# Linear attention and two MLPs: weights split once, their parts kept in DRAM, and the leaky ReLU taken by ScalarE out of PSUM

## The chip, the core and the metric

The kernel runs on one core of a Trainium2 chip. The metric is the device time of one execution in microseconds (us); lower is better. The engines have short names in all rows: PE is TensorE (matmuls), PEld its weight loads, DVE is VectorE, ACT is ScalarE, POOL is GpSimd, and SPq is the queue of SyncE, which issues all of this kernel's DMAs in a fixed order.

## The reference

For 4 batches of 576 tokens the reference does an attention without softmax over 8 heads and then two MLPs, all in float32:

```python
def phi(x):                                   # x: batch, head, 576, 64;  w_phi: 64 x 128
    proj = einsum('bhsd,df->bhsf', x, w_phi)
    proj = proj - max(abs(proj), axis=-1, keepdims=True)
    return concatenate([exp(proj), exp(-proj)], axis=-1)
q_p, k_p = phi(q), phi(k)
kv  = einsum('bhsf,bhsd->bhfd', k_p, v);  z = sum(k_p, axis=2)
x   = einsum('bhsf,bhfd->bhsd', q_p, kv) / (einsum('bhsf,bhf->bhs', q_p, z) + 1e-6)

h   = x @ w_in                                # 512 x 2048
x   = maximum(0.01 * h, h) @ w_out            # 2048 x 512
g   = x @ w_gate                              # 512 x 1536
out = (g / (1 + exp(-g)) * (x @ w_val)) @ w_out2
```

The weights reach the chip as float64.

## The kernel before

**Products in parts.** A float32 product is made of three fast ones: each operand is split into a high part (a rounding to the fast format `F32R`) and a low part (what is left), and high by high, high by low and low by high are added up in PSUM. A split is one ACT copy (the high part) and one DVE subtraction (the low part, `sub`, line 57).

**The two layers as units.** `products` (line 530 is its matmul) makes one unit: 24 matmuls of 128 x 128 by 288 columns, 12 for each half of the tokens of one batch. A batch has 16 units `u_l1` (first layer, one weight of 128 x 512 each), 12 pairs of `u_gate` and `u_val`, and after every four of `u_l1` or four such pairs a group of four units `u_out`, which read the four weights of that group (the sum, into `acc`). That makes 68 units per batch, 68 weights, and 6528 matmuls at line 530 in all. `u_l1` copies its product out of PSUM on ACT (`cp`, line 60), applies the leaky ReLU on DVE (line 554), and splits the result (`to_parts`, tile `gp`).

**A weight's way.** In batch 0 each of the 68 weights is loaded as float64 (`w_load`, line 477, into a buffer of the ring `wi`, which has 5), turned into float32 (`w_to_f32`: two ACT passes at lines 491 and 492, three DVE passes at 493, 494 and 499, into a buffer `wr`), and written to DRAM as float32 (line 504, `kept`). Then `w_split` (line 510 on ACT, line 57 on DVE) makes the two parts, for weights of the first kind again in a buffer of the ring `wi`, for the weights of `u_out` in a ring `wo`. In batches 1 to 3 the float32 copy is read back (line 480) and split again, once in each batch. Eight gate weights are turned into float32 ahead of time (`early`).

**The order.** Attention steps of the next batch are laid between the units of the present one; the first attention runs alone ahead of the first unit. `splits` calls loads, conversions and splits a fixed number of weights ahead. A scheduler then lays every engine's instructions into one fixed list; each engine and the DMA queue work their list strictly in order.

Of the kernel before, what the change touches and what calls it, by code (L numbers as in the profile page):

```python
# [7 lines left out]
F32 = mybir.dt.float32  # L8
# [9 lines left out]
P = 128  # L18
# [8 lines left out]
# blocks of 32 tokens in a half  # L27
NB = HT // 32
# columns of the constants before the signs
NC = P + 18 + NB  # L30
# token tiles of 128 rows; of tile i the first VAL[i] rows are its own, the rest belong to the next
# [3 lines left out]
# on the high word of a float64 read as float32, this takes 896 off the exponent  # L35
# [4 lines left out]
def linear_attention_two_mlps(ctx: ExitStack, tc, qT, kT, vt, w_phi, w1, w2, wg, wv, w3, cst, out):  # L40
# [21 lines left out]
    # ---------------------------------------------------------------- constants  # L62
# [30 lines left out]
    def bk(b=1):  # L93
        """A bank; those of the two layers still lie idle in the first attention's projections."""
        if b == 0:
            return T([P, 512], F32, "pm", 4, psm)
        return T([P, 512], F32, "pa", 4, psa)

    # ---------------------------------------------------------------- attention, keys
# [3 lines left out]
    def whole(b):  # L103
        """While the vector engine is short: whole float32 products in place of split ones."""
        return b < 2

    def lean(b):
        """Past the start, where the vector engine has time: the maxima from turned projections."""
        return b >= 1
# [139 lines left out]
    def k_steps(b):  # L249
        """Steps of the key side; each follows the one before by two on its data."""  # L250
# [32 lines left out]
    # ---------------------------------------------------------------- attention, queries  # L283
# [42 lines left out]
    def q_p(b, j, t):  # L326
        """Projections with features on the partitions, and their largest size by 32 features."""
# [12 lines left out]
    def q_m_t(b, j, t):  # L340
        """The largest over all features, as rows that one product takes off the projections."""
# [97 lines left out]
    def q_steps_t(b):  # L439
        """Steps of the query side: half the tokens of two heads take two for the projections,  # L440
        two for the exponentials and two for the products, one group behind the other."""
# [26 lines left out]
    # ---------------------------------------------------------------- weights  # L468
    wtile, w64, wf = {}, {}, {}
    src = {"1": w1, "2": w2, "g": wg, "v": wv, "3": w3}  # L470
    kept = {}

    def w_load(key, tag="wi", n=5):
        kind, b, f = key
        if b == 0 and (kind, f) not in kept:
            w64[key] = t = T([P, 512, 2], I32, tag, n)
            nc.sync.dma_start(out=t.rearrange("p n t -> p (n t)"), in_=src[kind][f].bitcast(I32))
        else:
            wf[key] = t = T([P, 512], F32, "wr", 4)
            nc.sync.dma_start(out=t, in_=kept[kind, f])  # L480

    def w_to_f32(key):
        """float64 bits to float32: sign, 31 bits, and the rounding, which goes onto the lower 16 bits
        (as they saturate, the step up is left out where all of them are set already)."""
# [4 lines left out]
        t = T([P, 512], F32, "wr", 4)  # L489
# [11 lines left out]
        kind, _, f = key  # L501
        uid[0] += 1
        kept[kind, f] = d = dram.tile([P, 512], F32, name=f"kept_{uid[0]}")
        nc.sync.dma_start(out=d, in_=t)

    def w_split(key):
        kind, b, f = key
        r = wf.pop(key)
        wtile[key] = t = T([P, 2, 512], F32R, *(("wo", 4) if kind in "23" else ("wi", 5)))
        i = act.activation(t[:, 0], r, AF.Copy)  # L510
        tc.stamp_issue_order_token(i.ins, "weights")
        sub(t[:, 1], r, t[:, 0].bitcast(F32))

    def early(key):
        """Weights that are made ready while the first attention runs."""
        w_load(key, "gp", 5)
        w_to_f32(key)
        del wf[key]

    # ---------------------------------------------------------------- the two layers  # L520
    gp, acc, x2h, x2l, sg = ({} for _ in range(5))

    def products(ops):
        """The two halves of the tokens, each in a bank of its own."""
# [25 lines left out]
    def u_l1(b, f):  # L550
        g = T([P, S], F32, "es", 5)
        for c, ps in products(in_ops(("1", b, f), xh, xl, b)):
            cp(g[:, c], ps)
        dve.scalar_tensor_tensor(out=g, in0=g, scalar=0.01, in1=g, op0=ALU.mult, op1=ALU.max)  # L554
# [219 lines left out]
```

## Time and profile before

| | |
|---|---|
| median of 3 runs | 1103.33 us (1102.61 to 1103.87) |
| span of the profiled execution, first to last instruction | 1099.4 us |
| PE busy | 1078.7 us, 98% of the span |
| DVE busy | 854.7 us, 78% |
| ACT busy | 659.9 us, 60% |
| moved by DMA | 130.25 MB, mean 118 GB/s |

The profiled execution has a span alone and no time of its own beside it; the median of the runs is 3.9 us above that span. A busy share is over the whole span. Since PE's matmuls are pipelined and their ends are modelled, PE counts as idle only where no matmul at all is under way.

### The profile page before, as it was taken

The numbers are of one execution on the slowest core, as the hardware profiler recorded it, in microseconds if no ns is written. First come the engines' busy times: TensorE is split into PE (matmuls) and PEld (weight loads), VectorE is DVE, ScalarE is ACT, GpSimd is POOL, SyncE is SP. The second block draws the span as 40 slices with busy tenths as digits, with TensorE's granted clock in tenths as the row PEclk, the third lists the DMA queues.
The fourth block names the chain that finished last, engine by engine and source line by source line (L and its number), as shares of the span: only waits on it lengthen the run. The fifth ranks groups of instructions, "written<-read, shape, count | busy, mean of one in ns | idle before, by whom it ended". The sixth has DMA issues, their size and how long they took to land.

```text
span 1099.4 us, 20402 instructions
## 1 busy us (share of the span) xinstructions
PE 1078.7 (98%) x7728; PEld 1041.9 (95%) x7728; DVE 854.7 (78%) x1765; ACT 659.9 (60%) x1457; POOL 6.8 (1%) x28
## 2 busy tenths in 40 slices
PE   7899999999999999999999999999999999999998
PEld 6668999999998999999999999999999999999998
DVE  6998889898999888779778888878787645565553
ACT  7768877667766787556646576655563444344421
POOL 1000000000000000000000000000000000000000
PEclk9999999999999999999999999999999999999999
DMA  9735766454654532223223322232131232323211
GB/s 332 237 93 174 213 209 194 154 155 155 211 185 125 172 100 91 80 57 110 62 76 108 103 73 89 77 98 97 36 97 51 80 99 77 92 82 106 97 48 44
DMA packets 69329, 130.25 MB, mean 118 GB/s; under 512 B 17136, under 2 KB 17392, under 8 KB 69232
## 3 DMA queue, kind: packets, MB, share of 16 engines
q1 hardware_dynamic: 69232, 128.95, 37.8%
q8 instruction: 61, 1.00, 0.4%
q14 instruction: 36, 0.29, 0.1%
HBM read 106.38 MB, written 22.54 MB: 117 GB/s over the span
## 4 chain that ended last, share of the span: by engine, by line
PE 82%; DVE 5%; DMA 5%; ACT 5%; issue 1%; SPq 0%; ACTq 0%; DVEq 0%
PE pm L530 70%; PE pa L391 4%; DMA wi<-in_w_dram 3%; PE pa L200 3%; PE pa L159 2%; DVE wr L499 1%; DMA wi<-in_wv_dram 1%; DVE wr L494 1%; ACT wr L491 1%; PE pm L299 1%; PE pa L344 1%; ACT wi L492 1%; PE pa L365 1%; PE pa L334 0%; PE pa L335 0%
## 5 line engine op out<-in xcount | busy, mean ns | idle before, releaser
L530 PE MATMUL pm<-xh,wi 128*128 128x288 f32 x2560 | 534.0, 297 | 2.2 <-ACT wi L510 1.6
L530 PEld LDWEIGHTS pm<-xh,wi 128*128 128x128 f32 x2560 | 416.5, 188 | 6.1 <-ACT wi L510 1.8
L530 PE MATMUL pm<-gp,wo 128*128 128x288 f32 x2688 | 385.3, 296 | 2.6 <-ACT acc L60 1.5
L530 PE MATMUL pm<-xl,wi 128*128 128x288 f32 x1280 | 378.9, 297 | 0.0
L530 PEld LDWEIGHTS pm<-gp,wo 128*128 128x128 f32 x2688 | 365.3, 188 | 6.6 <-ACT acc L60 1.8
L530 PEld LDWEIGHTS pm<-xl,wi 128*128 128x128 f32 x1280 | 240.4, 188 | 2.5 <-issue 1.7
L510 ACT ACTIVATE wi<-wr 128x512 fp32r<-128x512 f32 x160 | 101.0, 635 | 59.9 <-PE pm L530 34.6
L57 DVE TENSOR_TENSOR wi<-wr,wi 128x512 fp32r<-128x512 f32 x160 | 108.9, 682 | 14.2 <-ACT wi L510 13.0
L588 DVE TENSOR_TENSOR acc<-pm,acc 128x288 f32<-128x288 f32 x160 | 70.8, 453 | 57.1 <-PE pm L530 56.2
L510 ACT ACTIVATE wo<-wr 128x512 fp32r<-128x512 f32 x112 | 67.2, 630 | 65.5 <-PE pm L530 59.5
L57 DVE TENSOR_TENSOR wo<-wr,wo 128x512 fp32r<-128x512 f32 x112 | 74.3, 682 | 31.0 <-ACT wo L510 30.8
L57 DVE TENSOR_TENSOR gp<-es,gp 128x576 fp32r<-128x576 f32 x112 | 83.8, 749 | 13.5 <-ACT gp L60 12.6
L60 ACT ACTIVATE gp<-es 128x576 fp32r<-128x576 f32 x112 | 76.7, 687 | 25.0 <-DVE es L554 15.6
L561 ACT ACTIVATE es<-pm 128x288 f32<-128x288 f32 x96 | 39.4, 413 | 45.1 <-PE pm L530 44.5
L60 ACT ACTIVATE es<-pm 128x288 f32<-128x288 f32 x128 | 52.5, 417 | 16.5 <-PE pm L530 16.0
L57 DVE TENSOR_TENSOR fl<-ff,fh 128x512 fp32r<-128x512 f32 (+1 forms) x72 | 51.0, 714 | 13.0 <-ACT fh L60 12.7
L569 DVE SCALAR_TENSOR_TENSOR es<-pm,es 128x288 f32<-128x288 f32 x96 | 43.0, 450 | 23.0 <-PE pm L530 22.7
L492 ACT ACTIVATE wi<-wi 128x512 int32<-128x512 uint32 x60 | 41.2, 687 | 32.7 <-DMA wi<-in_w_dram 20.2
L562 DVE SCALAR_TENSOR_TENSOR es<-es,pm 128x288 f32<-128x288 f32 x96 | 42.1, 444 | 20.5 <-ACT es L561 19.9
L554 DVE SCALAR_TENSOR_TENSOR es<-es 128x576 f32<-128x576 f32 x64 | 48.0, 751 | 8.7 <-ACT es L60 8.7
L491 ACT ACTIVATE wr<-wi 128x512 f32<-128x512 f32 x60 | 40.7, 684 | 15.8 <-DMA wi<-in_w_dram 4.7
L394 ACT ACTIVATE dn<-pa 64x288 f32<-64x288 f32 x64 | 26.1, 408 | 37.8 <-PE pa L391 36.8
(108 smaller groups left out, 1282.1 us busy)
## 6 DMA issues: line engine op xcount, KB each, us to landing
wr<-kept SPq DMA_DIRECT2D x212, 256.0 KB, 2.8
wi<-in_w_dram SPq DMA_DIRECT2D x44, 512.0 KB, 4.3
kept<-wr SPq DMA_DIRECT2D x68, 256.0 KB, 4.1
wi<-in_wv_dram SPq DMA_DIRECT2D x12, 512.0 KB, 4.1
raw<-in_kT_dram SPq DMA_DIRECT2D x16, 288.0 KB, 3.1
raw<-in_qT_dram SPq DMA_DIRECT2D x16, 288.0 KB, 3.1
out_dram<-acc SPq DMA_DIRECT2D x16, 288.0 KB, 2.4
gp<-in_wg_dram SPq DMA_DIRECT2D x8, 512.0 KB, 7.8
```

The lines of the kernel that those rows point to most:

```text
L57: dve.tensor_tensor(out=o, in0=a, in1=b, op=ALU.subtract)
L60: act.activation(o, a, AF.Copy)
L391: pe.matmul(ps, w, x, start=(i == 0), stop=(i == len(ops) - 1))
L491: act.activation(t, high.bitcast(F32), AF.Abs, scale=REBIAS)
L492: act.activation(low, low.bitcast(U32), AF.Copy, scale=2.0**-29)
L510: i = act.activation(t[:, 0], r, AF.Copy)
L530: m = pe.matmul(ps, w, x[:, c], start=(i == 0), stop=(i == n - 1))
L554: dve.scalar_tensor_tensor(out=g, in0=g, scalar=0.01, in1=g, op0=ALU.mult, op1=ALU.max)
L561: act.activation(t[:, c], ps, AF.Tanh, scale=0.5)
L562: dve.scalar_tensor_tensor(out=t[:, c], in0=t[:, c], scalar=1.0, in1=ps, op0=ALU.add, op1=ALU.mult)
L569: dve.scalar_tensor_tensor(out=g[:, c], in0=ps, scalar=0.5, in1=g[:, c], op0=ALU.mult, op1=ALU.mult)
L588: dve.tensor_tensor(out=acc[o][:, t], in0=ps, in1=acc[o][:, t], op=ALU.add)
```

## The change

The weights are split only once, in batch 0, and what is written to DRAM is both parts (512 KB) in place of the float32 copy (256 KB). `keep_all_but(2)` writes them with a delay: the parts of a weight are written when two newer ones have been split. Batches 1 to 3 load the parts straight into a buffer of `wi` or `wo`, without a split. (The last two weights of batch 0 are still unwritten when batch 1 asks for them; these two are loaded as float64, converted and split a second time in batch 1.) The ring `wo` grows from 4 to 5 buffers, `wr` shrinks from 4 to 3. The leaky ReLU of `u_l1` becomes the function of the ACT pass that takes the product out of PSUM; the DVE pass is gone.

```diff
@@ weights
+    def parts_tile(key):
+        wtile[key] = t = T([P, 2, 512], F32R, *(("wo", 5) if key[0] in "23" else ("wi", 5)))
+        return t
+    def keep(cols, src_ap):
+        uid[0] += 1
+        d = dram.tile([P, cols], F32, name=f"kept_{uid[0]}")
+        nc.sync.dma_start(out=d, in_=src_ap)
+        return d
+    def keep_all_but(n):
+        while len(unkept) > n:
+            key, t = unkept.pop(0)
+            kept[key[0], key[2]] = keep(1024, flat(t))
     def w_load(key, tag="wi", n=5):
-        kind, b, f = key
-        if b == 0 and (kind, f) not in kept:
+        kind, _, f = key
+        if (kind, f) in kept:
+            nc.sync.dma_start(out=flat(parts_tile(key)), in_=kept[kind, f])
+        elif (kind, f) in ready:
+            wf[key] = t = T([P, 512], F32, "wr", 3)
+            nc.sync.dma_start(out=t, in_=ready[kind, f])
+        else:
             w64[key] = t = T([P, 512, 2], I32, tag, n)
             nc.sync.dma_start(out=t.rearrange("p n t -> p (n t)"), in_=src[kind][f].bitcast(I32))
-        else:
-            wf[key] = t = T([P, 512], F32, "wr", 4)
-            nc.sync.dma_start(out=t, in_=kept[kind, f])
...
     def w_split(key):
-        kind, b, f = key
+        if key not in wf:
+            return
         r = wf.pop(key)
-        wtile[key] = t = T([P, 2, 512], F32R, *(("wo", 4) if kind in "23" else ("wi", 5)))
+        t = parts_tile(key)
         i = act.activation(t[:, 0], r, AF.Copy)
         tc.stamp_issue_order_token(i.ins, "weights")
         sub(t[:, 1], r, t[:, 0].bitcast(F32))
+        unkept.append((key, t))
...
     def u_l1(b, f):
         g = T([P, S], F32, "es", 5)
         for c, ps in products(in_ops(("1", b, f), xh, xl, b)):
-            cp(g[:, c], ps)
-        dve.scalar_tensor_tensor(out=g, in0=g, scalar=0.01, in1=g, op0=ALU.mult, op1=ALU.max)
+            act.activation(g[:, c], ps, AF.Prelu, alpha=0.01)
         to_parts(g, ("1", b, f))
...
             ahead(loaded, w_load, done[0] + 5)
+            keep_all_but(2)
```

The scheduler makes other lists of it. Over the whole program ACT loses 202 splits and gains 2 conversions, DVE loses 202 splits and the 64 leaky passes; ACT has one table load in either list. Up to the last, eighth, low part of the first attention's result (`xl<-xf`) DVE's list held 17 conversions and 5 splits of weights and now holds 14 and 3.

The first place is ACT's list at the end of the first attention. `xh<-xf` takes a piece of its result, `dn` and `ff` are attention, `es<-pm` is the first unit's product; `wr<-wi` and `wi<-wi` convert a weight, `wr<-gp` one of the eight early ones, `wi<-wr` and `wo<-wr` split one. Before:

```order
L60 ACTIVATE xh_635<-xf_660 128x288
L394 ACTIVATE dn_724<-pa_732 64x288
L373 ACTIVATE ff_752<-pa_749 128x288
L374 ACTIVATE ff_752<-pa_749 128x288
L492 ACTIVATE wi_284<-wi_284 128x512
L510 ACTIVATE wi_294<-wr_273 128x512
L510 ACTIVATE wo_945<-wr_286 128x512
L394 ACTIVATE dn_758<-pa_755 64x288
L394 ACTIVATE dn_758<-pa_770 64x288
L491 ACTIVATE wr_1007<-wi_284 128x512
L60 ACTIVATE xh_745<-xf_742 128x288
```

And the same stretch now:

```order
L60 ACTIVATE xh_629<-xf_654 128x288
L513 ACTIVATE wr_756<-gp_754 128x512
L373 ACTIVATE ff_723<-pa_720 128x288
L374 ACTIVATE ff_723<-pa_720 128x288
L394 ACTIVATE dn_718<-pa_726 64x288
L373 ACTIVATE ff_746<-pa_743 128x288
L374 ACTIVATE ff_746<-pa_743 128x288
L394 ACTIVATE dn_752<-pa_749 64x288
L513 ACTIVATE wr_794<-gp_792 128x512
L60 ACTIVATE xh_739<-xf_736 128x288
```

Two splits and the conversion of a first-layer weight that stood here have moved behind the first unit; two of the early gate conversions stand here instead.

The second place is ACT's list late in batch 0, around the eleventh gate unit, whose product leaves PSUM in two halves (`es<-pm`). The split `wi<-wr` that feeds the very next unit stood ahead of the first half before:

```order
L510 ACTIVATE wi_4105<-wr_4084 128x512
L561 ACTIVATE es_4223<-pm_4224 128x288
L60 ACTIVATE gp_4187<-es_4115 128x576
L491 ACTIVATE wr_4190<-wi_4051 128x512
L561 ACTIVATE es_4223<-pm_4239 128x288
```

Now it stands between the halves:

```order
L60 ACTIVATE gp_4181<-es_4109 128x576
L580 ACTIVATE es_4219<-pm_4220 128x288
L529 ACTIVATE wi_4097<-wr_4078 128x512
L580 ACTIVATE es_4219<-pm_4235 128x288
L529 ACTIVATE wi_4146<-wr_4091 128x512
```

In batch 0 this late place (the split of the next unit's weight between the two halves or behind them, with no unit `u_out` coming first) occurs five times in the new list, at the fourth `u_l1` and at the third, eighth, eleventh and twelfth gate unit, and once in the old one, at the twelfth gate unit.

The third place is the DMA queue in the first layer of batch 0. `wi<-in_w_dram` is a float64 load, `kept` a write of a weight. Before:

```order
L504 DMA kept_1914<-wr_1908 128x512
L477 DMA wi_1906<-in_w_dram 128x1024
L504 DMA kept_1973<-wr_1967 128x512
L130 DMA raw_2594<-in_qT_dram 128x576
L504 DMA kept_2037<-wr_2031 128x512
L477 DMA wi_1919<-in_w_dram 128x1024
L477 DMA wi_1978<-in_w_dram 128x1024
```

And now:

```order
L483 DMA kept_2025<-wi_1899 128x1024
L483 DMA kept_2090<-wo_1957 128x1024
L483 DMA kept_2178<-wo_2020 128x1024
L130 DMA raw_2995<-in_qT_dram 128x576
L502 DMA wi_1902<-in_w_dram 128x1024
L502 DMA wi_1960<-in_w_dram 128x1024
L502 DMA wi_2023<-in_w_dram 128x1024
L502 DMA wi_2088<-in_w_dram 128x1024
```

The writes are twice as large, they read the parts' own buffers (`wi`, `wo`) in place of `wr`, and the float64 loads follow them in a bunch of four.

## Rows read from the trace of the kernel before

**Rows 1.** The page: span, and each engine's busy time, share and instructions.
```profile
span 1099.4 us, 20402 instructions
PE 1078.7 (98%) x7728; PEld 1041.9 (95%) x7728; DVE 854.7 (78%) x1765; ACT 659.9 (60%) x1457; POOL 6.8 (1%) x28
```

**Rows 2.** Busy time by stretch of the span; last: granted clock, DMA share, GB/s.
```profile
0.00:25.00 25.00, 19.11 (x76) 15.23 (x77) 16.56 (x49) 17.04 (x40) 2.84 (x15) 1.00 0.93 325
25.00:50.00 25.00, 22.93 (x105) 17.49 (x104) 22.63 (x56) 20.73 (x47) 2.04 (x7) 1.00 0.83 264
50.00:75.00 25.00, 21.91 (x101) 16.68 (x100) 24.52 (x64) 15.64 (x38) 0.00 (x0) 1.00 0.38 114
75.00:100.00 25.00, 23.58 (x127) 19.77 (x126) 18.51 (x46) 20.03 (x57) 0.48 (x2) 1.00 0.47 138
100.00:200.00 100.00, 100.00 (x701) 96.99 (x700) 90.30 (x180) 81.44 (x190) 1.39 (x6) 1.00 0.69 210
200.00:350.00 150.00, 145.21 (x1017) 137.47 (x1016) 138.61 (x302) 99.66 (x203) 0.00 (x0) 1.00 0.51 162
400.00:850.00 450.00, 450.00 (x3381) 443.07 (x3380) 367.81 (x750) 271.16 (x594) 0.00 (x0) 1.00 0.28 84
850.00:1050.00 200.00, 200.00 (x1508) 199.84 (x1507) 112.14 (x199) 85.38 (x174) 0.00 (x0) 1.00 0.30 91
1050.00:1099.40 49.40, 45.94 (x347) 45.71 (x345) 20.64 (x41) 8.85 (x17) 0.00 (x0) 1.00 0.12 41
```

**Rows 3.** The chain that ended last: start and length in us, what, instructions.
```profile
100.90 5.83 PE pm L530 x44
...
862.81 233.15 PE pm L530 x1756
```

**Rows 4.** Instruction groups: form and count | busy us, mean ns | idle before, releasers.
```profile
L57 DVE TENSOR_TENSOR wi<-wr,wi 128x512 fp32r<-128x512 f32 x160 | 108.9, 682 | 14.2 <-ACT wi L510 13.0
L510 ACT ACTIVATE wi<-wr 128x512 fp32r<-128x512 f32 x160 | 101.0, 635 | 59.9 <-PE pm L530 34.6 <-DMA wr<-kept 11.3 <-issue 10.2
...
L60 ACT ACTIVATE es<-pm 128x288 f32<-128x288 f32 x128 | 52.5, 417 | 16.5 <-PE pm L530 16.0
L554 DVE SCALAR_TENSOR_TENSOR es<-es 128x576 f32<-128x576 f32 x64 | 48.0, 751 | 8.7 <-ACT es L60 8.7
L499 DVE TENSOR_TENSOR wr<-wr,wi 128x512 uint16<-128x512 uint16 x60 | 44.8, 751 | 0.2
...
L494 DVE SCALAR_TENSOR_TENSOR wr<-wi,wr 128x512 int32<-128x512 int32 x60 | 40.6, 681 | 0.6
...
L493 DVE TENSOR_SCALAR wr<-wr 128x512 int32<-128x512 int32 x68 | 28.2, 417 | 12.4 <-ACT wr L491 12.4
```

**Rows 5.** The chain again, from 196 to 211 us.
```profile
196.69 5.37 DMA kept<-wr
...
202.15 1.26 ACT wr L491 x2
...
210.94 1.19 PE pm L530 x7
```

**Rows 6.** What PE waited for from 85 to 350 us: total, times, longest.
```profile
PE pm L530 <- ACT wi L510: 1.6, 1, 1.6
...
PE pm L530 <- DVE gp L57: 0.5, 1, 0.5
...
PE pm L530 <- DVE acc L588: 0.3, 1, 0.3
```

**Rows 7.** What the DMA queue waited for from 88 to 350 us.
```profile
SPq L477 <- PE pm L530: 51.6, 21, 5.8
...
SPq L477 <- DVE wr L499: 40.2, 18, 5.4
```

**Rows 8.** DMA issues: times, KB each, median us from issue to landing.
```profile
wr<-kept SPq DMA_DIRECT2D x212, 256.0 KB, 2.8
wi<-in_w_dram SPq DMA_DIRECT2D x44, 512.0 KB, 4.3
```

More of the change, by code (lines that the diff above doesn't have):

```diff
@@ L470, in linear_attention_two_mlps, with flat @@
     src = {"1": w1, "2": w2, "g": wg, "v": wv, "3": w3}
-    kept = {}
-    def w_load(key, tag="wi", n=5):
-        kind, b, f = key
-        if b == 0 and (kind, f) not in kept:
+    kept, ready, unkept = {}, {}, []
+    def parts_tile(key):
+        wtile[key] = t = T([P, 2, 512], F32R, *(("wo", 5) if key[0] in "23" else ("wi", 5)))
+        return t
+    def flat(t):
+        return t.rearrange("p a n -> p (a n)").bitcast(F32)
+    def keep(cols, src_ap):
[7 more added lines that the diff above has]
+            kept[key[0], key[2]] = keep(1024, flat(t))
+    def w_load(key, tag="wi", n=5):
+        kind, _, f = key
[5 more added lines that the diff above has]
+        else:
             w64[key] = t = T([P, 512, 2], I32, tag, n)
             nc.sync.dma_start(out=t.rearrange("p n t -> p (n t)"), in_=src[kind][f].bitcast(I32))
-        else:
-            wf[key] = t = T([P, 512], F32, "wr", 4)
-            nc.sync.dma_start(out=t, in_=kept[kind, f])
     def w_to_f32(key):
@@ L488, in w_to_f32 @@
         low, high = r[:, :, 0], r[:, :, 1]
-        t = T([P, 512], F32, "wr", 4)
+        t = T([P, 512], F32, "wr", 3)
         ti = t.bitcast(I32)
@@ L500, in w_to_f32 @@
         wf[key] = t
[L501 to L504, printed above, removed]
     def w_split(key):
-        kind, b, f = key
+        if key not in wf:
+            return
         r = wf.pop(key)
-        wtile[key] = t = T([P, 2, 512], F32R, *(("wo", 4) if kind in "23" else ("wi", 5)))
+        t = parts_tile(key)
         i = act.activation(t[:, 0], r, AF.Copy)
@@ L517, in early @@
         w_to_f32(key)
-        del wf[key]
+        ready[key[0], key[2]] = keep(512, wf.pop(key))
     gp, acc, x2h, x2l, sg = ({} for _ in range(5))
```

## The prediction

> **What bounds the kernel now.** I read the busy shares first, then the same by stretch, then the chain that ended last, then the waits. PE is busy 1078.7 of 1099.4 us [rows 1]; only 20.7 us are left to win in which no matmul is under way. The stretches show where they lie [rows 2]. Ahead of 100 us, in the first attention, PE idles 12.5 us: 5.9 in the first slice of 25 us, where it waits for its first data, then 2.1, 3.1 and 1.4. From 100 to 200 us, in the first layer of batch 0, it idles not at all. From 200 to 350 us, in the gate and value units of batch 0, it idles 4.8 us. From 400 to 1050 us it is busy all the time, and 3.5 us are the tail behind the last sums (49.40 less 45.94). So the kernel has a first third, up to 350 us, where the preparation of weights and the attention can hold PE up, and two thirds in which PE is the wall.
>
> Behind the wall the pace is fixed. In the chain 1756 matmuls of line 530 take 233.15 us in the last batch, 132.8 ns each; in the first layer of batch 0 a run of 44 takes 5.83 us, 132.5 ns each [rows 3]. Around the first of these DVE is busy 56% and DMA moves 91 GB/s, around the second DVE is busy 90% and DMA moves 210 GB/s [rows 2]. The pace hangs on neither, and the granted clock is 1.00, the 2.4 GHz level, in all rows. 6528 matmuls at 132.6 ns are 866 us that the change can't touch.
>
> **The change part by part.**
>
> *Batches 1 to 3, splits and leaky ReLU gone.* 202 splits at 635 ns of ACT and 682 ns of DVE [rows 4] (those of `wo` I take at the same price) are 128 and 138 us; 48 leaky passes of 751 ns are 36 us of DVE. All of it lies beside PE's solid stretch from 400 to 1050 us. Gain 0, and also 0 as a bound, since PE has no idle time there to give back.
>
> *Batches 1 to 3, loads twice as large.* 202 loads grow from 256 to 512 KB. A load of 256 KB lands 2.8 us after its issue; the float64 loads have the new size, and land after 4.3 us [rows 8]. The traffic from 400 to 850 us roughly doubles from 84 GB/s, against 325 GB/s in the first slice [rows 2]. The tight place is the ring `wo`: at the end of a group of sums four of five buffers come free at once, and the next group reads its four weights, of which three are still to be loaded, four units later, at least 4 x 24 x 132.6 ns = 12.7 us. Side by side the three need 4.3 us plus two times 1.6 us (512 KB at 325 GB/s), 7.5 us. Cost 0, with 5.2 us of cover; strictly one behind the other they would need 12.9 us and the cover would be gone. The two weights converted again in batch 1 hide in the same stretch.
>
> *First attention.* Ahead of its last result DVE has 3 conversions less, at 417 + 681 + 751 = 1849 ns, and 2 splits less: 5.5 + 1.4 = 6.9 us [rows 4]. From 50 to 75 us DVE is busy 24.52 of 25 us [rows 2], so what it does there sets the pace, and a shorter list should pull the first unit forward. It can't gain more than PE's idle time from 25 to 100 us, 6.6 us, and at worst gains nothing, if the path through ACT and PE is as long. I take 3.1 us, the idle time of the one slice in which DVE never rests.
>
> *First layer of batch 0.* The moved work comes back here: +6.9 us of DVE. The 16 leaky passes of batch 0 leave: 16 x 751 ns = 12.0 us. DVE's 90.3 of 100 us [rows 2] becomes about 85, so PE, which never idles here, should still not. ACT's pass out of PSUM is there before and after (417 ns [rows 4]), now with another function; I take it at the same time. Cost 0; without the 12.0 us DVE would be at 97 of 100 and this stage would begin to hold PE up.
>
> The Trainium skill speaks against this last edit: its page "ScalarE: Activation LUTs", section "Rules for kernel authors", sends relu and max to VectorE and not to ScalarE. The row of 417 ns says that ACT makes this pass anyway, and the same page's account of the pipeline, one element per cycle per lane whatever the function, would leave it there; by the rule the 12.0 us would stay on DVE, the first attention's gain would be lost, and the sum below would be 1102.5 us.
>
> *Writes no longer hold `wr`.* At 196.69 us a write of a float32 copy takes 5.37 us; ACT's conversion waits for that buffer until 202.15 us, and the chain goes on from it to PE at 210.94 us [rows 5]. On its way PE loses 0.5 us behind `gp` and 0.3 us behind `acc` [rows 6]. Now `wr` is free as soon as its split is done. Gain 0 to 0.8 us; I take 0.8.
>
> *Writes now hold `wi` and `wo`.* This is the new wait. A float64 load in batch 0 waits for a buffer of `wi` already: 51.6 us in 21 waits for PE to finish a unit, 40.2 us in 18 for a conversion [rows 7]. A part's buffer may now be used again only when its write has landed too. The writes are twice as large, stand two weights behind, and the loads follow in a bunch. Behind them in the queue stand the float64 loads, and behind these the conversions and splits for which PE waits. No row shows this wait. Its lower bound is 0: a write issued two weights after the split (at 68 weights in the 262 us from 88 to 350 us, some 7.7 us later) and landed 4.3 us after that is gone 12 us after the split, about when a unit three places on has been computed (3 x 3.2 us plus attention). For the upper bound, a split that came late cost PE 1.6 us at once [rows 6]; the split now stands late at five units in batch 0, where it stood so at one. Four more of these are 6.4 us. In the first layer three conversions fewer lie ready, but DVE has time. I take 0, since the one row for a late split comes behind a late float64 load and not from its place alone, and keep 6.4 us for the range.
>
> Sum: 3.1 + 0.8 = 3.9 us off the span of 1099.4 us, 1095.5 us. The median of the runs lies 3.9 us above that span, so the forecast is 1103.3 - 3.9 = 1099.4 us.
>
> **The rivals.** A measurement of this kernel tells about 0.2%, 2.2 us, from no change; faster means under 1101.1, slower over 1105.5 us.
>
> *Nothing moves.* The first attention's chain runs through ACT and PE as much as through DVE, the idle time stays, and only the 0.8 us or less is won: 1102.5 to 1103.3 us. For it: PE's stalls there are many and small, and DVE is not full after 75 us. Against it: 24.52 of 25 us.
>
> *The ring `wi` decides, slower.* The writes keep part buffers, float64 loads start later, and PE meets a split that isn't done. Price 1.6 us at each of four more units, with the gain of the start eaten, since PE merely arrives earlier at the same wait: 1103.3 + 6.4 = 1109.7 us. With half of the gain kept it is about 1107. It decides from the point where a write lands behind the last matmul of its unit. For it: the 91.8 us of waits for this ring, and the five late places. Against: DVE's 12.0 us, and a stage that lost nothing before.
>
> *Late parts in batches 1 to 3.* If the three loads for `wo` run one behind the other with one more between, they take 17.2 us against 12.7: 4.5 us at nine groups of first-layer sums, 40 us, 1140 us. If they are just not covered, 0.2 us at nine groups, 1.8 us, 1101. Against it: the queue issues such loads without waiting for their landing.
>
> *All of it comes back.* The 6.6 us and the 4.8 us of idle time vanish: 1103.3 - 11.4 = 1091.9 us.
>
> *The pace itself.* If traffic of DVE and ACT slowed each matmul, 202 splits less would speed up 6528 of them. The two runs of 132.8 and 132.5 ns at 56% and 90% of DVE speak against it. The page "TensorE: Matmul & The Clock Gate" of the Trainium skill, section "Back-to-back issue gap", gives 122.5 ns for 288 columns; the trace differs with 132.6. If the 10 ns between were contention and all went, 65 us would be gone and the time would be 1038 us.
>
> **How the numbers follow.** Forecast 0.43 (of it 0.36 under 1101.1 us; its own range 1096 to 1102.5). Nothing moves 0.24 (0.04 faster, 0.19 same, 0.01 slower). The ring decides 0.23 (0.03 same, 0.20 slower). Late parts 0.04, slower. All comes back 0.05 and the pace 0.01, faster. That is 0.46 faster, 0.29 same, 0.25 slower. The range leaves out below the last two (0.06), above the late parts and the upper half of the ring's case (0.14): 1094.5 to 1108.5 us.
>
> **What would show it.** In the profile of the changed kernel, right: from 25 to 100 us PE's idle time falls from 6.6 to about 3.5 us; from 100 to 200 us PE stays solid with DVE near 85; no conversion waits for a write; from 400 us on PE has no idle time and still takes 132.6 ns a matmul, while DVE falls under 65% there; loads of parts land after some 4.3 us. Wrong, and how: PE idle between 88 and 350 us behind `wi` (split) with the float64 loads waiting for a `kept` write; PE idle behind a DMA into `wo` after 350 us; the start no earlier although DVE has less to do; or an ACT pass of the leaky ReLU longer than 417 ns.

## The result and the profile after

The changed kernel takes 1115.26 us (median of 4 runs, 1112.22 to 1116.18) beside 1103.13 us for the kernel before on the same chip: a ratio of 1.0106 (95% interval 1.0090 to 1.0122). It is slower by 1.1%, where 1099.4 us and a small gain were forecast. The profiled execution took 1116.18 us with a span of 1114.3 us.

The page of the changed kernel, beside [rows 1]:

```profile
span 1114.3 us, 19823 instructions
PE 1084.8 (97%) x7728; PEld 1047.4 (94%) x7728; DVE 708.7 (64%) x1505; ACT 564.4 (51%) x1259; POOL 6.6 (1%) x28
```

DVE has 146 us less to do and ACT 95 us less, as intended, and the end comes 14.9 us later. The span splits into PE's idle and busy time. Idle went from 20.7 to 29.5 us, which is 8.8 us; busy went from 1078.7 to 1084.8 us with the same 7728 matmuls, which is 6.1 us. Together they are the 14.9 us. So there are two losses to find: stalls, and matmuls that run slower.

The busy time by stretch, in the columns of [rows 2]:

```profile
0.00:25.00 25.00, 19.80 (x80) 15.70 (x81) 17.47 (x51) 18.00 (x41) 3.07 (x15) 1.00 0.94 331
25.00:50.00 25.00, 21.71 (x102) 17.23 (x100) 20.27 (x49) 18.82 (x43) 1.66 (x6) 1.00 0.76 240
50.00:75.00 25.00, 22.89 (x110) 18.26 (x109) 22.84 (x58) 14.56 (x36) 0.00 (x0) 1.00 0.32 100
75.00:100.00 25.00, 23.39 (x128) 19.48 (x127) 18.65 (x48) 19.21 (x54) 0.52 (x2) 1.00 0.39 122
100.00:200.00 100.00, 98.40 (x680) 93.92 (x679) 80.87 (x161) 80.05 (x189) 1.35 (x5) 1.00 0.77 271
200.00:350.00 150.00, 139.28 (x937) 130.80 (x935) 135.28 (x289) 98.00 (x198) 0.00 (x0) 0.97 0.69 235
350.00:400.00 50.00, 48.52 (x355) 47.99 (x355) 35.17 (x76) 30.35 (x76) 0.00 (x0) 0.97 0.75 262
400.00:850.00 450.00, 450.00 (x3386) 443.43 (x3385) 294.11 (x616) 225.29 (x505) 0.00 (x0) 1.00 0.43 150
850.00:1050.00 200.00, 200.00 (x1509) 199.97 (x1509) 61.92 (x120) 51.52 (x105) 0.00 (x0) 1.00 0.50 172
```

From 400 us on PE is solid as before. The first 100 us hold 12.2 us of idle time, where there were 12.5. Everything else lies from 100 to 400 us, the stage in which batch 0 converts its weights: 13.8 us idle where there were 4.8, and a granted clock below 1.00, which appears nowhere in the rows of before.

What PE waited for from 100 to 400 us, to be read beside [rows 6] (total, times, longest, in us):

```profile
PE pa L334 <- ACT ff L374: 4.4, 3, 3.2
PE pa L365 <- DVE mrow L354: 2.5, 1, 2.5
PE pm L550 <- ACT wo L529: 1.5, 1, 1.5
...
PE pa L391 <- DVE xf L409: 1.3, 1, 1.3
```

Lines 334, 365 and 391 are attention steps of the next batch, and line 550 is the units' matmul. By what came last, PE mostly waits not for weights but for attention, and one wait is 3.2 us long. The chain that led to it (start and length in us, what):

```profile
298.93 5.03 DMA wi<-in_w_dram
...
304.05 0.69 ACT wi L514
304.75 0.41 ACT dn L394
...
305.48 0.41 ACT ff L374
...
305.94 0.61 PE pa L334
306.54 0.24 PE pa L335
306.78 0.24 PE pm L550
```

At 304.05 us a conversion (L514) stood at the head of ACT's list and waited for its float64 load. The exponentials of the attention (L374) stood behind it, and PE behind them. But this chain ends last by only 0.7 us. DVE, busy 5.00 of 5 us, wrote the low part of the present unit's own weight no earlier than this:

```profile
304.51 0.68 DVE L57 TENSOR_TENSOR wi<-wr,wi 128x512 fp32r<-128x512 f32 x1
```

Behind the attention step, the next matmul of the unit needs that low part, which is done at 305.19 us. So PE would have stood for some 2 us with the exponentials in time as well: the split was late too. The last two rows of the chain show a second thing: matmuls of 288 columns now start 0.24 us apart, where 0.1326 us is usual. The stretches around it, in the columns of the view above:

```profile
300.00:305.00 5.00, 2.78 (x18) 2.23 (x16) 5.00 (x11) 2.94 (x7) 0.00 (x0) 0.98 0.83 258
305.00:310.00 5.00, 4.06 (x17) 4.07 (x18) 4.55 (x10) 4.99 (x12) 0.00 (x0) 0.50 0.65 240
310.00:315.00 5.00, 5.00 (x30) 4.79 (x30) 3.39 (x9) 2.33 (x5) 0.00 (x0) 0.84 0.50 125
```

Behind the 3.2 us stall the granted clock is 0.50, the 1.2 GHz level, and then 0.84 in the mean: 0.50 x 5 + 0.16 x 5 = 3.3 us more of full-speed time are gone, or 2.8 us if only PE's busy 4.06 us of the first stretch are counted, so that this one stall costs nearly twice its length. By stretches of 25 us the granted clock is 0.93, 0.86 and 0.93 in three of the twelve from 100 to 400 us and 1.00 in the others, 7.0 us in all, which is about the 6.1 us of longer busy time.

What the DMA queue waited for from 100 to 350 us, beside [rows 7], and the landing times, beside [rows 8]:

```profile
SPq L502 <- DVE wr L521: 52.4, 21, 7.3
SPq L483 <- DVE wi L57: 45.0, 21, 9.5
SPq L502 <- DMA kept<-wi: 18.9, 7, 4.8
```

```profile
wi<-kept SPq DMA_DIRECT2D x120, 512.0 KB, 3.5
wo<-kept SPq DMA_DIRECT2D x82, 512.0 KB, 5.4
wi<-in_w_dram SPq DMA_DIRECT2D x46, 512.0 KB, 5.0
```

Two suspects are in these rows. Float64 loads (line 502) wait 18.9 us for writes that still hold their `wi` buffer, the wait of the rival "the ring `wi` decides" (the expectations call it the ring theory). And they land after 5.0 us, not 4.3, with more traffic about (the traffic theory). Both are there, and the experiments show that neither is the main cause.

### The profile page after: what moved, and what is told of

It reads as the page before. It is cut to its first block, busy times and chain, and to the rows that moved or that the text cites. A ratio compares the mean times of both kernels' runs of the same rounds, so it can differ in the third digit from the quotient of the medians.

```text
span 1114.3 us, 19823 instructions
## 1 busy us (share of the span) xinstructions
PE 1084.8 (97%) x7728; PEld 1047.4 (94%) x7728; DVE 708.7 (64%) x1505; ACT 564.4 (51%) x1259; POOL 6.6 (1%) x28
## 4 chain that ended last, share of the span: by engine, by line
PE 85%; DMA 5%; DVE 4%; ACT 4%; issue 1%; SPq 0%; ACTq 0%; DVEq 0%
PE pm L550 72%; PE pa L391 4%; PE pa L200 3%; DMA wi<-in_w_dram 2%; PE pa L159 2%; PE pm L299 1%; DVE wr L521 1%; PE pa L334 1%; PE pa L344 1%; PE pa L238 1%; PE pa L365 1%; DMA wi<-in_wv_dram 1%; DVE wr L516 1%; PE pa L335 1%; PE pa L370 0%
## 5 line engine op out<-in xcount | busy, mean ns | idle before, releaser
L550 PE MATMUL pm<-gp,wo 128*128 128x288 f32 x2688 | 389.5, 296 | 1.7 <-ACT wo L529 1.5
L514 ACT ACTIVATE wi<-wi 128x512 int32<-128x512 uint32 x62 | 43.0, 693 | 31.9 <-DMA wi<-in_w_dram 18.8
L60 ACT ACTIVATE fh<-ff 128x512 fp32r<-128x512 f32 (+1 forms) x72 | 47.5, 663 | 0.9
L200 PE MATMUL pa<-ff,pk 128*128 128x256 f32 (+1 forms) x160 | 43.0, 384 | 4.0 <-issue 3.0
L521 DVE TENSOR_TENSOR wr<-wr,wi 128x512 uint16<-128x512 uint16 x62 | 46.2, 752 | 0.6
L60 ACT ACTIVATE acc<-pm 128x288 f32<-128x288 f32 x64 | 26.0, 422 | 33.4 <-PE pm L550 33.2
L516 DVE SCALAR_TENSOR_TENSOR wr<-wi,wr 128x512 int32<-128x512 int32 x62 | 42.3, 686 | 0.9
```

Source lines behind the costliest of these rows:

```text
L60: act.activation(o, a, AF.Copy)
L200: pe.matmul(ps[:, 256 * h : 256 * h + 256], v[:n, h].rearrange("p a d -> p (a d)"), part[b, j, s][:n, h].rearrange("p a f -> p (a f)"), st ...
L514: act.activation(low, low.bitcast(U32), AF.Copy, scale=2.0**-29)
L516: dve.scalar_tensor_tensor(out=ti, in0=high, scalar=-0x80000000, in1=ti, op0=ALU.bitwise_and, op1=ALU.bitwise_or)
L521: dve.tensor_tensor(out=t16, in0=t16, in1=e16, op=ALU.add)
L550: m = pe.matmul(ps, w, x[:, c], start=(i == 0), stop=(i == n - 1))
```

## The experiments

They are grouped by what they ask. Every edit makes the scheduler write new lists, so each run also has a rival that the expectations call the theory of the order or of the lists: the new list is worse by itself, whatever the edit was for. "Idle" is the length of a stretch less PE's busy time in it, from the view by stretch of each run. The kernel before has 6.6 us from 25 to 100 us and 4.8 us from 100 to 400 us; the changed one 7.0 and 13.8.

### The two halves of the change

The leaky ReLU alone, on the kernel before (leaky_only):

```diff
-            cp(g[:, c], ps)
-        dve.scalar_tensor_tensor(out=g, in0=g, scalar=0.01, in1=g, op0=ALU.mult, op1=ALU.max)
+            act.activation(g[:, c], ps, AF.Prelu, alpha=0.01)
```

> The kernel before with the leaky ReLU on ScalarE alone; weights are converted, written and split as before. Ring theory (writes that hold the part buffers of wi make the float64 loads of batch 0 late): nothing is held longer here, DVE has 64 passes of 751 ns less, so 1099 to 1103.5 us and PE idle from 100 to 400 us at most the 4.8 us of before. Rival, the new function or the new order of the lists costs the time: 1108 us or more, with PE idle of 10 us or more between 100 and 400 us.

Measured: ratio 1.0005 (0.9992 to 1.0018), idle 7.0 and 5.1 us. This half is worth nothing in either direction. The rest, with the leaky pass on DVE again (parts_only):

> The changed kernel with the leaky ReLU back on DVE. Ring theory: the loss of 12 us comes from the weights' edit, so it stays, and 12.0 us more of DVE work in batch 0 adds to it: 1114 to 1122 us, with float64 loads waiting for writes from wi as in the changed kernel. Rival, the ScalarE pass costs the time: back to 1101 to 1105 us.

Measured: ratio 1.0142 (1.0110 to 1.0175), idle 7.0 and 13.5 us. The loss comes with the weights.

### More room in the ring, and more traffic without the change

The change with six buffers of `wi` and, for want of room, four of `es` (wi6_es4):

> The changed kernel with 6 buffers in the ring wi in place of 5; the room comes from the ring es, 4 in place of 5. Ring theory: the float64 loads no longer wait for the writes (19.7 us of waits in the changed kernel fall under 5), PE's idle time from 100 to 400 us falls from 13.8 to under 7 us and the granted clock stays at 1.00: 1099 to 1106 us. Rival, the doubled traffic makes loads slow whatever buffers there are: 1112 to 1116 us, with float64 loads still at 5.0 us to landing. A fourth buffer less in es may cost up to 2 us by itself.

Measured: 1.0077 (1.0052 to 1.0101), idle 8.6 and 11.2 us. Somewhat better, but most of the idle time stays. The queue still waits 16.1 us for writes that hold `wi`, where under 5 were expected, so this run didn't take the suspected wait away. Then the kernel before with its writes doubled, first all of them (before_write512), then all but those of the eight early gate weights (before_write512_l, whose edit is shown):

```diff
...
-        nc.sync.dma_start(out=d, in_=t)
+        n = 1 if kind == "g" and f < 8 else 2
...
+        copies = t.rearrange("p (o n) -> p o n", o=1).to_broadcast([P, n, 512])
+        nc.sync.dma_start(out=d, in_=copies)
```

> The kernel before with every write of a float32 copy made twice as large (the same 256 KB written two times by one DMA, 512 KB); all else as before. It has the changed kernel's traffic of writes in batch 0, but wi and wo are not held by it. Ring theory: the traffic is not the cause, so 1103 to 1107 us (wr is held longer, which adds a little to the 0.8 us seen before). Rival, traffic: 1110 us or more, with float64 loads landing after 5 us in place of 4.3.

> The kernel before, its writes doubled to 512 KB, but not those of the eight gate weights that are made ready in the first attention (the earlier run with all doubled lost 6 us there). The clean price of the traffic. Ring theory: ratio 1.000 to 1.004, idle time of 100 to 400 us 5 to 8 us, no stretch at the lower clock level. Traffic theory: ratio 1.007 to 1.012, idle time over 10 us, loads of float64 weights landing after 5 us or more.

Measured: 1.0131 (1.0095 to 1.0166) with idle 12.8 and 7.1 us, and 1.0112 (1.0093 to 1.0132) with idle 14.4 and 6.4 us. The ratio alone would have fitted the traffic theory; the places don't. From 100 to 400 us the doubled writes cost about 2 us. The loss is in the first attention, where a conversion must wait for the write that still holds its `wr` buffer, 7.5 us in place of 1.5 in the kernel before (the clean variant, ACT's waits from 20 to 100 us):

```profile
ACT wr L491 <- DMA kept<-wr: 7.5, 4, 2.9
```

### Writes taken away, and writes that hold another ring

Only the first weight's parts are written, and batches 1 to 3 load that one copy every time (one_write):

```diff
-            kept[key[0], key[2]] = keep(1024, flat(t))
+            if not kept:
+                kept["first"] = keep(1024, flat(t))
+            kept[key[0], key[2]] = kept["first"]
```

> The change, but the parts of the first weight alone are written to DRAM; batches 1 to 3 load this one copy 202 times, so their weights are wrong and their traffic is the same. Order theory (the splits that stand late, the instructions in another order): the loss stays, ratio 1.007 to 1.011, 100 to 400 us idle by more than 10 us. Theories of the ring and of the traffic alike: no write holds a buffer of wi and none takes part of the DMA, the idle time of 100 to 400 us falls from 13.8 to 3 to 6 us, the clock stays up, float64 loads land after 4.3 to 4.5 us, ratio 0.996 to 1.001.

Measured: 1.0108 (1.0090 to 1.0126), idle 6.8 and 13.2 us. This run decides against both suspects at once. The stretch from 100 to 400 us, and what PE waited for in it:

```profile
100.00:400.00 300.00, 286.76 (x1983) 273.68 (x1982) 250.44 (x525) 208.57 (x465) 1.39 (x5) 0.98 0.42 138
```

```profile
PE pm L552 <- ACT wi L531: 6.0, 6, 3.1
PE pa L334 <- ACT ff L374: 2.8, 2, 2.2
PE pa L365 <- DVE mrow L354: 2.4, 1, 2.4
```

The DMA moves 138 GB/s here in place of 252, no buffer of `wi` or `wo` but the first weight's is held by a write, and PE still idles 13.2 us; what is late are now the splits themselves (line 531). As the main cause, the ring fell with this, and the traffic with it.

The other half of the pair writes the same 512 KB, but out of the float32 weight, with four buffers of `wr` (writes_from_wr):

```diff
...
-        t = T([P, 512], F32, "wr", 3)
+        t = T([P, 512], F32, "wr", 4)
...
-        unkept.append((key, t))
+        twice = r.rearrange("p (o n) -> p o n", o=1).to_broadcast([P, 2, 512])
+        uid[0] += 1
+        d = kept[key[0], key[2]] = dram.tile([P, 1024], F32, name=f"kept_{uid[0]}")
+        nc.sync.dma_start(out=d.rearrange("p (o n) -> p o n", o=2), in_=twice)
...
-            keep_all_but(2)
```

> The change, but the 512 KB are written out of the float32 weight in wr (twice the same 256 KB, as soon as the split has read it; wr has 4 buffers again), so the second parts of batches 1 to 3 are wrong. The traffic is that of the change, wi and wo are free when their unit is computed. Ring theory: ratio 0.998 to 1.004, idle time of 100 to 400 us 4 to 8 us, no wait of the queue for a write that holds wi. Traffic theory: ratio 1.008 to 1.012, as with the change, and idle time over 10 us. A new wait for wr behind its write would show as waits of the conversions on ACT or DVE, worth 1 to 3 us.

Measured: 1.0120 (1.0099 to 1.0140), but idle 16.1 us in the start and only 5.3 us from 100 to 400 us. It moved full traffic through that stage without harm there. One thing that it shares with the kernel before and not with one_write was the fourth buffer of `wr`, which the change had given up. That made the new theory: a conversion can start only into a free `wr` buffer, and with three of them conversions run less far ahead of the splits.

### An unneeded buffer more

The kernel before with a sixth buffer of `wi`, alone (before_wi6) and with the leaky pass on ACT (leaky_wi6):

> The kernel before with the leaky pass on ACT and a sixth buffer of wi; the parts stay as they were. If float64 loads that come late for want of a wi buffer cost the kernel before its 4.8 us of idle time from 200 to 350 us: 1097 to 1099 us, ratio 0.996 to 0.998. If that idle time comes from DVE's and ACT's work in that stretch and not from the loads: ratio 0.999 to 1.001.

> The kernel before with a sixth buffer of wi, which can only take waits away; the scheduler writes a new list for it. Theory of the lists: it loses nonetheless, 1.003 to 1.01, with idle time in the first attention, where the buffer isn't needed, 8 us or more from 25 to 100 us against 6.6. If an unneeded buffer does no harm: 0.997 to 1.001.

Measured: 1.0083 (1.0068 to 1.0098) and 1.0052 (1.0036 to 1.0067) with the leaky pass. From 100 to 400 us the buffer helped: idle 3.4 and 2.6 us, the lowest with all writes in place. But both lost in the first attention, with 11.5 us idle and a mean granted clock of 0.92 from 25 to 100 us. The scheduler had used the room to put more conversions there: 19 end ahead of 100 us, where the kernel before has 17.

### The third buffer, tested

The change, and the kernel that writes only once, each with four buffers of `wr` and nothing else altered:

```diff
-            wf[key] = t = T([P, 512], F32, "wr", 3)
+            wf[key] = t = T([P, 512], F32, "wr", 4)
...
-        t = T([P, 512], F32, "wr", 3)
+        t = T([P, 512], F32, "wr", 4)
```

> The change with 4 buffers of wr, as before, in place of 3; nothing else. Theory of the conversions' room (a conversion can start only when one of the wr buffers is free, and the change took one away, so conversions and with them float64 loads run less far ahead): idle time of 100 to 400 us falls from 13.8 to 5 to 8 us, clock at the upper level, ratio 1.000 to 1.005. Ring theory (writes hold wi): nothing changes there, ratio 1.008 to 1.012, waits of the queue on kept writes near 20 us. Theory of the lists (each new list of instructions that the scheduler writes is worse than that of before by an amount of its own): any value from 1.003 to 1.012, with the idle time in another place than with 3 buffers, the first attention among them.

> The kernel in which only the first weight's parts are written, with 4 buffers of wr (weights of batches 1 to 3 wrong as there). Theory of the conversions' room: 0.998 to 1.002, since neither writes nor the third buffer are left to hold anything up; idle time of 100 to 400 us 3 to 6 us. If the room alone were not the cause: 1.007 to 1.012 again, idle time over 10 us.

> The change with each write issued right behind its split instead of two weights later. Ring theory: each buffer is held some 7 us less, the waits of the queue on kept writes fall from 20 to under 8 us, ratio 1.003 to 1.007. Theory of the conversions' room: the waits on the writes fall too, but the idle time stays over 10 us, ratio 1.008 to 1.012.

| buffers of `wr` | parts of | ratio (interval) | idle 25-100 | idle 100-400 |
|---|---|---|---|---|
| 3 (the change) | all written | 1.0106 (1.0090-1.0122) | 7.0 | 13.8 |
| 3 (delay0) | all written, no delay | 1.0112 (1.0086-1.0138) | 6.8 | 12.2 |
| 3 (one_write) | one written | 1.0108 (1.0090-1.0126) | 6.8 | 13.2 |
| 4 (after_wr4) | all written | 1.0075 (1.0054-1.0096) | 9.7 | 5.9 |
| 4 (one_write_wr4) | one written | 0.9994 (0.9984-1.0004) | 9.1 | 2.8 |

The delay changes nothing that can be told, though it took little of the suspected wait away (the queue's waits for writes are 15.7 us in delay0 and 18.9 in the change). The fourth buffer takes the idle time of the middle stage from 13.8 to 5.9 us and from 13.2 to 2.8 us, and the clock stays up there. The stretch from 100 to 400 us of after_wr4, and its first wait of PE:

```profile
100.00:400.00 300.00, 294.10 (x2079) 282.72 (x2077) 253.18 (x531) 214.65 (x485) 1.88 (x7) 1.00 0.72 251
```

```profile
PE pm L550 <- ACT wi L529: 3.8, 3, 2.8
```

None of the attention steps 334, 365 and 391 is among its waits any more, at the same traffic (251 GB/s) and with the same writes. (With the conversions further ahead, the queue waits only 6.2 us for writes that hold `wi`, in place of 18.9; one_write, where that wait is gone and the idle time isn't, says that this follows the fourth buffer and is not what it acts by.) ACT still waits for float64 loads, 27.6 us in all in place of 31.2, but not so long at a time, and the queue waits less for conversions to give their `wi` buffer free. ACT's costliest wait of that kind in the changed kernel, from 100 to 350 us (the queue's stands above, 52.4 us in 21 waits, the longest 7.3), and then both with the fourth buffer:

```profile
ACT wi L514 <- DMA wi<-in_w_dram: 16.4, 12, 5.9
```

```profile
ACT wr L513 <- DMA wi<-in_w_dram: 8.0, 6, 2.7
ACT wr L513 <- DMA wi<-in_wv_dram: 7.1, 3, 3.7
ACT wi L514 <- DMA wi<-in_w_dram: 7.0, 5, 2.7
```

```profile
SPq L502 <- DVE wr L521: 32.9, 14, 4.3
SPq L502 <- DMA kept<-wi: 6.2, 2, 3.7
```

What the room does can be worked out from the traces. For the 40 weights of `wi` in batch 0, take the time from the end of the split's low part to the first matmul of its unit. Its median is 10.4 us in the kernel before, 3.3 in the changed one and 10.1 in after_wr4; 2.9 in one_write and 11.0 in one_write_wr4. From the end of a conversion to the start of its split the medians are 5.9, 2.2 and 5.0 us, then 2.7 and 5.6. So with three buffers a split is done about one unit (3.2 us) ahead of its use, and little stands between a late load or a full engine and PE.

What is left of after_wr4's loss is in the first attention: 9.7 us idle and a granted clock of 0.93. A chain there, which ended in a stall of 2.3 us:

```profile
71.77 3.41 DMA wi<-in_w_dram
...
75.28 0.20 ACT wi L514
...
75.96 0.41 ACT ff L373
...
82.34 0.33 DVE xf L409
...
82.80 0.72 PE pa L370 x2
```

It is the figure of 304 us again, in another place: a conversion at the head of ACT's list waits for its load, with the attention's exponentials behind it. On its way to PE the chain also passes DVE's own conversion steps (L515, L516 and L521, 1.3 us). The kernel has 17 conversions ahead of 100 us here, 14 with three buffers.

The writes are not free either, once the fourth buffer is there. after_wr4 and one_write_wr4 differ by them alone, 1.0075 against 0.9994: of the 8.8 us between their spans 3.1 are idle time from 100 to 400 us, and about 5 are the lower clock in the first attention. Whether the latter comes from the writes or from the new list isn't shown.

### What is left with four buffers

Delay 0 and delay 4 with four buffers (after_wr4_d0, after_wr4_d4), five buffers of `wr` and four of `es` (after_wr5_es4), and fewer gate weights made ready in the first attention, with four buffers (after_wr4_pre6, after_wr4_pre4) and with three (after_pre6):

```diff
-    pre, made, start = 8, 0, 30
+    pre, made, start = 6, 0, 30
```

> The change with 4 buffers of wr and each write right behind its split. What is left of the loss with 4 buffers lies in the first attention (9.7 us idle from 25 to 100 us, and a stretch at the lower clock level), where the delay changes nothing but the list. Theory of the lists: the idle time of 100 to 400 us stays at 3 to 7 us, that of the start is drawn anew, ratio anywhere from 0.998 to 1.010. Theory of the writes (they hold buffers or take DMA time, and with 4 buffers of wr that is what is left): ratio under 1.004, with the queue's waits on kept writes halved.

> The same with the write four weights behind, so that each buffer is held longer. Theory of the lists: idle time of 100 to 400 us 3 to 7 us again, ratio from 0.998 to 1.010 by what the start does. Theory of the writes: ratio 1.010 or more, idle time of 100 to 400 us over 9 us, waits of the queue on kept writes over 25 us.

> The change with 5 buffers of wr and 4 of es (5 of each don't fit). If room for conversions is what batch 0 lacks: idle time of 100 to 400 us 2 to 5 us (5.9 with 4), ratio 0.999 to 1.006, the start decides. If the fourth buffer was enough or es is short now: 6 us or more, with waits of DVE or ACT for es in batch 0.

> The change with 4 buffers of wr and six gate weights made ready in the first attention instead of eight. If the conversions that stand in the first attention cost it the 9.7 us of idle time there (one at the head of ACT's list that waits for its float64 load holds up the exponentials behind it), the idle time of 25 to 100 us falls to 6 to 8 us, the clock stays up, and the ratio is 0.999 to 1.004. If the start is a matter of the list's luck alone, the idle time stays at 9 to 12 us or more, ratio 1.005 to 1.012.

> The change with 4 buffers of wr and four gate weights made ready in the first attention. If fewer conversions in the start go on paying: idle time of 25 to 100 us under 8 us, the four conversions more in batch 0 hide there, ratio 0.997 to 1.001, a version better than the kernel before. If what they save in the start comes back from 100 to 350 us, where DVE is near 90% busy: idle time of 100 to 400 us over 8 us, ratio 1.002 to 1.008.

> The change as it is (3 buffers of wr) with six gate weights made ready in the first attention. If the third buffer is the cause by itself, the idle time of 100 to 400 us stays over 10 us and the ratio is 1.007 to 1.012 here as well; if the number of early weights did it, as 1.0018 with four buffers might be read, the ratio falls to 1.002 to 1.005.

| kernel | ratio (interval) | idle 25-100 | idle 100-400 | conversions begun by 100 us |
|---|---|---|---|---|
| after_wr4_d0 | 1.0080 (1.0063-1.0098) | 9.9 | 6.4 | 17 |
| after_wr4_d4 | 1.0097 (1.0081-1.0113) | 10.1 | 5.6 | 17 |
| after_wr5_es4 | 1.0148 (1.0123-1.0174) | 11.0 | 10.9 | 18 |
| after_wr4_pre6 | 1.0018 (1.0004-1.0032) | 8.0 | 5.4 | 15 |
| after_wr4_pre4 | 1.0009 (0.9995-1.0023) | 4.9 | 7.8 | 14 |
| after_pre6 | 1.0180 (1.0154-1.0206) | 7.0 | 20.4 | 12 |

The delay is again no matter that can be told (the queue's waits for writes are 6.4, 6.2 and 5.1 us with delays of 0, 2 and 4). Fewer early conversions free the start, and with four buffers the middle stage pays little for it: eight, six and four early weights give 1.0075, 1.0018 and 1.0009. With three buffers the same edit makes it worse: after_pre6 idles 20.4 us in the middle stage, after_wr4_pre6 5.4. after_wr4_pre4 and the changed kernel both have 14 conversions begun at 100 us, and one idles 7.8 us from there to 400 us, the other 13.8. This pair alone doesn't tell the room from the lead at 100 us, for of the 14 only six are weights of the first units in the changed kernel (the others are early gate weights), and ten in after_wr4_pre4. But by 150 us the changed kernel has 27 conversions behind it and after_wr4 28, and most of the idle time comes after 200 us; so the room counts from then on. In after_wr5_es4 the shorter ring `es` is a second edit. Its splits end a median of 15.7 us ahead of their units, the longest of the changed kernel's versions, so the 10.9 us don't come from want of room. wi6_es4, the other kernel with four buffers of `es`, has a median of 9.0 us there and idles 11.2; whether `es` is what costs in these two wasn't tried by itself.

after_wr4_pre4 undoes the loss of the change, 1.0% of it, but doesn't beat the kernel before; no version here does by more than its measurement can tell. The best, one_write_wr4, leaves out nearly all writes and gains nothing over the kernel before that the interval shows.

## Why the prediction was wrong, point by point

- **PE is the wall from 400 us: right.** 450.00 of 450 and 200.00 of 200 us are busy, 1509 matmuls in the last 200 us, 132.5 ns each. The 202 splits less gave nothing back, the loads of 512 KB (3.5 and 5.4 us to land) hid, and the rivals "late parts" and "the pace itself" are out. The latter was priced by the wrong line: the Trainium skill's page "TensorE: Matmul & The Clock Gate", section "Back-to-back issue gap", gives the formula behind 122.5 ns for a single matmul by itself and not for a stream.
- **The leaky ReLU on ACT, cost 0: right.** `ACT es<-pm` takes 417 ns with the new function as before, and the edit alone makes 1.0005. The Trainium skill, on its page "ScalarE: Activation LUTs", section "Rules for kernel authors", would keep such a pass on VectorE; these two numbers don't bear that out here, nor do they show a gain from leaving VectorE.
- **First attention, -3.1 us: mis-sized.** Idle from 25 to 100 us stayed at 7.0 us against 6.6, so that the part of the rival "nothing moves" that speaks of the start was right. DVE did let go where it was full, from 24.52 to 22.84 of 25 us from 50 to 75 us, and PE idled 1.0 us less in that slice; but in the slice before it PE lost 1.2 us. The mechanism isn't void: between lists of the changed kernel, with 17 and 14 conversions (after_wr4 and the change), the idle time there is 9.7 and 7.0 us. But the kernel before had its 6.6 us with 17 already, and no new list of the changed kernel with 17 came down to it (9.1 to 10.1 us, and 16.1 in writes_from_wr).
- **Writes no longer hold `wr`, -0.8 us: not seen.** From 100 to 350 us no conversion waits for a write of `wr` any more (2.3 us in 2 waits of ACT before), but the ring that was freed so is the one that was cut, and nothing of a gain can be told apart beside that.
- **Writes now hold `wi` and `wo`, 0: not what decided, on weak grounds.** The wait is there (18.9 us in 7 waits of the queue). But with nearly all writes gone the loss stays at 1.0108 and the idle time from 100 to 400 us at 13.2 us against 13.8; with four buffers they cost 3.1 us there (5.9 against 2.8). With delays of 0, 2 and 4 weights the ratios lie at 1.0112 and 1.0106 (three buffers), 1.0080, 1.0075 and 1.0097 (four). The rival "the ring `wi` decides" had the sign right and named 1109.7 us; its mechanism is not the main cause, so that this was luck.
- **First layer of batch 0, cost 0, and no term for the cut of `wr`: the step that failed.** The prediction judged the stage by DVE's busy share ("three conversions fewer lie ready, but DVE has time") and left out that `wr` shrinks from 4 to 3 buffers; that edit stands in the sum only by what it frees. DVE did have time in the first layer (80.87 of 100 us, where about 85 were forecast), and PE idled 1.6 us there all the same; the larger loss, 10.7 us against 4.8, lies from 200 to 350 us in the gate and value units, and 1.5 us more up to 400 us. With a buffer less, splits end a median of 3.3 us ahead of their units in place of 10.4; late loads and splits then reach PE, at once or through the attention that stands behind them in ACT's list. Measured: +9.0 us of idle time from 100 to 400 us, of which the fourth buffer gives 7.9 back. In the total it gives back less, 1.0106 to 1.0075, because the new list loses in the start.
- **A cost with no term at all: the clock.** Some 7 us of full-speed time went with the stretches at the lower level behind stalls, 6.1 by PE's longer busy time. Even the bound of 6.4 us (four late splits at 1.6 us) counted a stall by its own length.

What stays open: why new lists with 17 conversions ahead of 100 us idle 9 to 10 us in the start, without doubled writes, where the old one and that of leaky_only idle 7. Each edit makes the scheduler write a new list; the old list with a new edit wasn't tried. So a single ratio can carry a scatter as large as 0.8% (before_wi6) that has nothing to do with the edit's purpose. Open as well is by which wait the room acts when nothing is written: the queue's wait for conversions, which the fourth buffer shortened in the change, is 74.3 us in one_write and 97.8 us in one_write_wr4, where it grew. The missing buffer itself stands above the scatter. In four pairs that differ by it alone it takes the idle time from 100 to 400 us from 13.8 to 5.9 us, 13.2 to 2.8, 12.2 to 6.4 and 20.4 to 5.4. Of all kernels with five buffers of `es`, the five with three buffers of `wr` idle 12.2 to 20.4 us there, and the thirteen with four 2.6 to 7.8 us.

## What to carry to other kernels

A buffer taken from a ring is a term of the sum like any instruction: ask what runs ahead through that ring, and price the stage in which it must, even if every engine there has time. When a chain shows a wait (here: for a write), take its cause away before believing it; the wait went and the loss stayed. And where a scheduler lays the instructions out anew for every edit, compare stretches and not totals, and judge a cause by several lists with it and several without.

## What the runs showed of the hardware that was not expected

A stall of TensorE can cost nearly twice its length: behind the 3.2 us at 302.8 us the granted clock was 0.50, the 1.2 GHz level, matmuls of 288 columns started 0.24 us apart instead of 0.1326, and about 3 us more were lost. The kernel before had no such stretch (granted clock 1.00 in all rows, its longest wait in the stage 1.6 us), while one buffer more in `wi` was enough to bring one into its first attention. From 75 to 90 us of before_wi6:

```profile
75.00:80.00 5.00, 1.92 (x10) 1.13 (x8) 5.00 (x12) 2.06 (x5) 0.00 (x0) 1.00 0.53 137
80.00:85.00 5.00, 3.75 (x13) 2.70 (x14) 3.76 (x10) 2.56 (x6) 0.00 (x0) 0.63 0.79 231
85.00:90.00 5.00, 5.00 (x18) 3.83 (x17) 3.71 (x8) 4.96 (x12) 0.00 (x0) 0.68 0.14 52
```

PE was busy 1.92 of 5 us, and in the next 10 us ran at 0.63 and 0.68. So a list without stalls is worth more than the sum of its waits says.
